# A shifted long convolution beside linear attention: four tap sums by adding DMA instead of two, and a new written-out order

## The chip, the core and the metric

The kernel runs on one core of a Trainium2 chip, and the metric is the device time of one execution in microseconds (us). A core has five engines that each work through a queue of their own in order: TensorE (PE, matrix products and transposes), VectorE (DVE), ScalarE (ACT), GpSimd (POOL) and SyncE (SP, which here only issues DMAs). They share an on-chip memory of 128 partitions (SBUF) and eight banks of accumulators (PSUM, here `ps_all`). Transfers between the chip's memory (HBM) and SBUF, or within SBUF, run on 16 DMA engines. They are issued on SP's queue or, where the transfer adds to its destination, on POOL's.

## The reference

Two independent functions of separate inputs, all in bf16, put side by side: the output is 2048 rows of 576 + 576 columns.

```python
# part A: inputs q, k, v (2048 x 576), shift_k (576 x 4), ssm_k (576 x 2048), ssm_D (576)
for t in range(4):
    k_shift = k_shift + k_pad[:, t:t+S, :] * shift_k[:, 3 - t]
kv = k_shift * v
y = irfft(rfft(kv, 2S) * rfft(ssm_k, 2S))[:S]        # causal convolution with a filter of 2048
y = y + kv * ssm_D
a = q * y
# part B: inputs x (2048 x 576), wqkv (576 x 1728), wo (576 x 576); 32 heads of 18
q, k, v = split(x @ wqkv)
phi = lambda t: where(t > 0, t + 1, exp(t)) + 1e-6
pq, pk = phi(q), phi(k)
kv = einsum("bhsd,bhse->bhde", pk, v);  z = sum of pk over s
num = pq @ kv;  den = pq . z + 1e-6
b = (num / den) @ wo
```

## The kernel before, in words

**Part A.** The 576 channels are worked on in three chunks of 192 (0, 1, 2), and the 2048 positions as 128 partitions of 16 neighbours, in two halves of 8. The shifted k of one chunk and one half is a *conv piece* (`conv_piece`, stages cv00 to cv21: the first digit is the chunk, the second the half). A piece is two tap products on DVE (L402, 3072 elements a partition each: a tap makes two of the four shifted products at once), a first sum that adds one tap's 3072 elements to the other's ("tap+"), a second sum of 1536, and the product with v ("tapv", 1536). The three after the taps are recorded as an operation of either VectorE or GpSimd (L236). For the pieces that the list `ACC` names, the first sum is instead a DMA inside SBUF that adds to its destination, issued by GpSimd (L408). All conv pieces of half 0 read k from the buffer kh0, those of half 1 from kh1, and multiply into v0 and v1.

The long convolution is a Fourier transform done in two matmul stages each way. First the filter: its rows hs0 to hs4 are loaded, transposed by PE ("htr") and evicted ("hev") into hT, with ssm_D added to the first sample ("hD"). For each chunk, "s1" multiplies by the table G (8 groups of 4 matmuls, L468), DVE or ACT evicts it, DVE transposes blocks of 32 ("tr"), "s2" is 4 groups of small matmuls (L516), evicted again. The chunk's three thirds are numbered 3*chunk + 0, 1, 2. kv goes the same way (s1u, s2u); then the two spectra are multiplied (p1, p2, on DVE or POOL, with X, a copy of the filter's spectrum with neighbouring partitions exchanged, made by two DMAs), "i1" (L552) and "i2" (L577) transform back with the table E, the result is evicted to yb, multiplied with q ("yq") and stored.

**Part B.** x is loaded in four groups, as rows (x_sb) and transposed (xT; group 0 by PE, groups 1 to 3 by transposing DMAs). "k r" (16 of them, L624) projects keys of 128 positions, ACT takes an exponential ("kexp", L629), and DVE joins it with the linear branch into pk ("kphi", L632). "q" (20 of them, L645) does the same for queries into pqT. G (10 groups, L674) is x transposed times pk; from it and the value weights follow per head kv (L709, masked by DVE at L712, "kvev") and the sums z, "den" and their reciprocals, which are stored to HBM ("rw") and loaded back spread over partitions (rb), and multiplied into pqT ("pqn", L236). M is kv times wo ("M", evicted at L231; a correction for the 1e-6 in "msf" and "msev"); "out" (32 groups, L814) multiplies pqT by M, is evicted and stored.

**The order.** Nothing is scheduled at build time. Every operation is recorded with a running number (838 in all), and two long strings fix the rest: `PLAN` gives the order of all of them with a letter for the engine, and `PLACES` the SBUF offset or PSUM bank of each of 473 buffers, so that buffers whose times don't overlap share a place, and the later one's first write waits for the earlier one's last reader.

```python
def _issue(P):
    names = dict(P="PE", A="ACT", D="DVE", G="POOL", S="SP")
    for w in PLAN.split():
        o = P.ops[int(w[1:])]
        o.eng = names[w[0]]
```

So D84 is operation 84 on DVE, and G84 would be the same on POOL. Each engine takes its own operations in this order, and an instruction that waits holds up all behind it on its engine. SP keeps some eight of its DMAs under way. One rule is added at the end: a two-input operation (`two=1`: sums and products) on POOL waits for the last such operation that stands before it in `PLAN` on DVE, so that these don't run at once.

Numbers that are spoken of later: loads 54 and 53 (the tail of the key weights wk, 72 KB, and their main part), 56 and 55 (of the query weights wq), 18 (srow, the tap weights), 26 and 28 (x group 0), 41, 46, 51 (transposed x), 58 to 60 (kh0), 62 (kh1), 61 and 63 (v0, v1), 365, 371, 423, 472, 478 (hs0 to hs4); 27, 29, 39, 44, 49 (the copies "x4c" of x columns); the conv pieces

| piece | taps | first sum | second sum | tapv |
|---|---|---|---|---|
| cv00 | 64, 65 | 66 | 67 | 68 |
| cv01 | 69, 70 | 71 | 72 | 73 |
| cv10 | 74, 75 | 76 | 77 | 78 |
| cv11 | 79, 80 | 81 | 82 | 83 |
| cv20 | 84, 85 | 86 | 87 | 88 |
| cv21 | 89, 90 | 91 | 92 | 93 |

95 + 3r, 96 + 3r, 97 + 3r (projection, exponential and kphi of key block r: P110, P116, P134 and D121, D130, D136, D139 are such), 143 to 202 the same for queries (D163, P182), 203 to 227 G, 228 to 245 kv, z, den, 246 to 271 the reciprocals' way, 272 to 284 M, msf and msev, 285 to 364 out, 365 to 526 the filter's transform (P507 is an s2 of chunk 2), 527 to 763 kv's transform and the products (P697 is an s1 of chunk 2), 764 to 835 i2 and the end.

Of the kernel before, what the change touches and what calls it, by code (L numbers as in the profile page):

```python
# [22 lines left out]
YA = [0, 1]  # L23
XD = [1, 2, 3]
HDT = []
ACC = [(0, 1), (2, 1)]
HP = [0, 128, 256, 384, 480, 576]


# [154 lines left out]
def kernel(  # L184
# [39 lines left out]
    def load(name, b, fn, nb, row, wr=None, rd=(), after=(), engs="S"):  # L224
        return P.op(engs, fn, rd=rd, wr=[b] if wr is None else wr, name=name, after=after, nb=nb, row=row)
# [165 lines left out]
    def conv_piece(cc, bh):  # L391
# [12 lines left out]
        for i in (0, 2):  # L404
            P.op("D", lambda e, i=i: tap(e, i), rd=[kh, (Wj, 0)] + ([(Wj, 1)] if cc else []), wr=[(m, i)], name="tap",
                 n=3072, x2=1, two=1, st=st)
        if (cc, bh) in ACC:
            load("acc", m, lambda e: nc.gpsimd.dma_start(  # L408
# [459 lines left out]


PLAN = """  # L870
G8 D836 P837 G5 G57 S26 G13 S28 G6 D27 S16 S54 S53 G3 P30 D29 D31 G11 G7 P36 P32 S21 S365 G1 G9 A33 S371 S20 G2 P34
P98 S423 D35 S19 P95 P368 G0 D37 A15 A99 A369 S18 S41 P366 D100 G228 D367 P101 P375 A96 S472 D97 P372 A102 A377
A374 D376 P394 G4 D373 S59 D370 A395 P386 P392 D103 G10 G14 P384 P426 D387 A393 P424 G12 S56 G378 D385 A23 D427
P388 A425 P433 D379 G42 A434 P435 P382 S55 G428 D389 D436 P390 P380 P437 D391 A383 P443 D438 A381 P429 D405 P475
P441 A444 P431 D414 S24 S40 S58 P473 A430 A442 D396 P439 A432 A440 S60 P146 P417 A147 P415 S25 A474 G477 D476 D445
A418 P104 D148 A105 P143 S46 P401 P397 A416 P446 P448 S51 D106 P452 A144 P155 A449 A453 A398 D454 A402 P149 P152
A156 A150 D145 A447 S478 P408 D463 G47 D157 A153 P403 P399 P457 D151 A409 D400 S50 S45 P468 P170 A458 A404 P406
D469 P410 P461 D154 A462 D65 P459 P421 P161 A171 A411 P158 S48 A460 P412 S43 P466 P455 G52 D172 P419 D64 A407 A422
P164 D75 A456 P481 D74 D66 P470 A413 A467 P464 S230 P450 A420 P167 A165 G67 A451 A471 A162 D163 P479 A465 A480 A168
P197 D166 P200 A482 P191 A159 A192 D169 A201 D160 A198 D202 D193 P110 P185 D76 A111 G44 G483 D112 D199 P173 S594  # L880
A186 P134 P176 A174 G49 S61 D175 D187 A135 P122 A177 P179 G77 D178 D136 P107 S652 P119 A123 D124 A180 A108 P137 D78
D85 S229 A120 P188 D109 D181 A138 S595 D121 G68 S232 A189 P140 P128 S38 A141 D139 D190 P125 D84 A129 D142 P131 D130
P486 D86 P116 A126 A487 A132 A117 D127 P113 G87 S231 A114 S62 A39 S653 D133 D118 P194 P494 P182 D115 A183 P223 D88
A224 P484 A485 A195 D70 D79 A495 P226 A225 S17 P208 D69 D80 A227 S63 P236 D237 D238 P203 G71 D184 P239 D196 P243
P488 G81 D204 A209 A205 A210 P492 D240 D241 S552 D244 P498 A489 P206 D242 D245 A493 P490 A499 D72 D73 A491 P496
S553 S246 P218 A497 S247 A207 D219 P537 D220 A538 P531 S259 P529 A530 P221 P533 D82 S260 S258 P527 A532 A222 S254
D83 A534 P535 D89 A536 S261 P213 A528 P618 S265 P620 P608 P211 D90 A621 P610 A609 P606 D255 A212 D619 D266 A611
P614 D214 S269 G91 G270 P216 A607 D500 S252 P503 A215 P507 G262 A615 D518 P519 D509 P612 D217 A504 D508 P616 A520
D92 S263 S674 P541 P233 A613 P539 A617 A542 S271 A540 D93 P699 D235 P281 G272 D234 S267 P693 D700 P275 D694 A282
P273 P279 A276 A274 P277 D280 S248 A278 P691 A692 P685 P695 P283 D622 A696 S256 D686 P687 D284 S673 P629 P516 G253  # L890
A688 P627 P514 D517 P697 G264 D564 A630 P689 G268 A698 P332 A333 P347 A628 P355 A690 D664 G249 P357 P350 A356 A515
A351 P667 P669 D348 P671 A358 D585 S250 D701 A672 S631 P521 P512 G251 P505 P330 P352 A670 P327 P325 A513 A331 A668
D522 D353 A328 P665 D506 S573 P510 S574 D743 S22 P706 A326 P625 S329 P525 A666 P501 A511 P623 D643 A624 G257 P300
P345 S359 A707 P340 A626 P342 A341 A526 P302 P750 P704 P748 D502 P648 S354 G675 S632 A346 D301 P590 A343 D722 P650
G676 D705 D591 P362 S711 A649 D363 P360 P312 P567 A303 D651 A749 P565 A751 S731 P644 A361 S732 P523 D313 P646 A568
P744 S349 P708 A524 P315 D543 S753 D316 P310 P337 P317 D647 P569 A745 D311 S334 P586 D634 P725 A566 A645 S304 D655
P571 P723 A709 A338 P727 S364 A318 A728 P290 A726 S344 A587 P320 P683 A321 P307 A570 S319 A572 S314 D724 P729 P746
D291 A684 P702 P550 P548 D654 A703 P677 A747 P305 P660 P681 A306 A308 A661 D633 P641 S752 A682 P292 A551 P658 A293
A549 A659 P335 A642 D576 P679 A680 P297 A678 P635 D730 P546 P592 P544 D754 D755 D733 A336 S710 P588 D734 D713 A636
A593 A589 P756 P637 D712 A545 P295 A638 P639 A640 D298 P656 P737 A657 P739 A740 P662 A547 A738 A663 P741 P718 P720  # L900
P758 A721 P760 A759 P762 D757 P800 A801 A761 P735 D575 D555 S294 S94 P794 D296 A795 P796 D597 P802 D763 S339 A742
P577 D719 A803 A797 A736 D596 P806 S309 P716 P788 P714 A717 D554 P579 D804 A807 D798 P322 P808 A715 P824 P826 P790
S299 A323 D825 P832 A789 A791 P600 S324 P560 A809 A601 S799 A827 P581 A833 P812 P562 D792 P598 A599 D578 P814 D582
A561 D815 P830 A580 G810 G828 A563 S793 D813 P583 A584 D831 D816 S805 P558 P820 D821 G834 D559 P602 P556 S811 P818
P604 P285 D819 D603 A557 S829 S835 A605 D822 S817 D286 S823 P287 A288 S289 P784 P782 D785 A783 D786 P776 S787 A777
P778 A779 P772 D773 D780 S781 P764 P770 P766 D767 A771 D774 S775 A765 D768 S769
"""
PLACES = """
# [16 lines left out]
"""  # L925


# [28 lines left out]
```

## Time and profile before

| | |
|---|---|
| median of 3 runs | 160.50 us (160.44, 160.50, 160.75) |
| profiled execution | 161.04 us, of which the span of engine work is 159.2 us |
| mean granted TensorE clock | 0.994 |
| HBM read, written | 20.86 MB, 4.99 MB: 162 GB/s over the span |
| adding DMAs (GpSimd's queue) | 1.57 MB, 5.6% of the 16 DMA engines' span |

The profile is of one execution. Its first part gives each engine's busy time, its share of the span and its instructions; a stage is a stretch of the span that I chose by its bounds, written start:end and followed by its length and the busy time in it. The groups of instructions are listed by code line, engine, operation, output and inputs, with count, total busy time and the mean of one in ns. In the chain, each entry is a start, a time and the instruction. The busy time of PE is no proof that it is the limit at each place, because an engine that is nearly always busy can still start its work late; that is why stages and chain are read beside it. SPq and POOLq are the queues' issuing of a DMA.

### The profile page before, as it was taken

To read this page: it belongs to the slowest core of one execution; us is meant where nothing else is said; L and a number is where in the kernel's file an instruction comes from. 1 tells how busy PE (TensorE), PEld (TensorE's weight loads), DVE (VectorE), ACT (ScalarE), POOL (GpSimd) and SP (SyncE) were. 2 spreads that over 40 slices of the span, in tenths; PEclk is the share of its full clock that TensorE was granted. 3 is DMA by queue.
4 is the path that set the end of the run, shared out by engine and by line. 5 is a ranking of instruction groups with operands and counts; after the bars stand their busy time and mean duration, and the time that the engine had idled before them with its cause. 6 is when DMAs were issued, how large, how long until landed. Compare 5 with 4: busy or idle time off the path is not lost.

```text
span 159.2 us, 4176 instructions
## 1 busy us (share of the span) xinstructions
PE 150.4 (94%) x1663; PEld 119.5 (75%) x1663; DVE 143.3 (90%) x183; ACT 122.7 (77%) x224; POOL 63.2 (40%) x51
## 2 busy tenths in 40 slices
PE   6897899999999999999999999999999999999970
PEld 2686785545677889787888878787777889999960
DVE  1537999999999999899899999999999999998981
ACT  3148799999996566561869599899989999896860
POOL 8901100110199170606920594996891000004400
PEclk9999999999999999999999999999999999999997
DMA  5999699999999128496925597891647449415575
GB/s 164 301 401 291 155 218 377 214 200 277 397 371 302 31 36 296 197 252 213 164 81 183 155 161 234 268 368 67 245 171 252 174 120 408 178 43 161 151 211 148
DMA packets 26317, 34.37 MB, mean 216 GB/s; under 512 B 15802, under 2 KB 20923, under 8 KB 25530
## 3 DMA queue, kind: packets, MB, share of 16 engines
q1 hardware_dynamic: 25754, 32.54, 65.8%
q0 software_dynamic: 544, 1.57, 5.6%
q8 instruction: 13, 0.21, 0.5%
q14 instruction: 6, 0.05, 0.1%
HBM read 20.86 MB, written 4.99 MB: 162 GB/s over the span
## 4 chain that ended last, share of the span: by engine, by line
PE 82%; DVE 5%; DMA 3%; ACT 3%; issue 2%; SPq 1%; DVEq 1%; ACTq 0%
PE ps_all L645 13%; PE ps_all L814 13%; PE ps_all L624 12%; PE ps_all L674 12%; PE ps_all L552 10%; PE ps_all L468 9%; PE ps_all L516 5%; PE ps_all L577 4%; DMA wk<-in_B_wqkv_dram 3%; DVE Cu L231 2%; PE ps_all L437 2%; SPq L222 1%; ACT sph L229 1%; PE ps_all L709 1%; DVE q L236 1%
## 5 line engine op out<-in xcount | busy, mean ns | idle before, releaser
L645 PE MATMUL ps_all<-xT,wq 128*126 128x512 bf16 (+1 forms) x100 | 24.0, 381 | 0.1
L814 PE MATMUL ps_all<-M,pqT 126*128 126x288 bf16 (+1 forms) x160 | 22.1, 287 | 0.0
L236 POOL TENSOR_TENSOR m<-m 128x1536 bf16<-128x1536 bf16 (+1 forms) x4 | 15.5, 3885 | 15.4 <-DVE m L236 15.4
L624 PE MATMUL ps_all<-wk,xT 128*128 128x288 bf16 x160 | 21.1, 286 | 0.5 <-DMA wk<-in_B_wqkv_dram 0.5
L402 DVE TENSOR_TENSOR m<-kh,Wj 128x3072 bf16<-128x3072 bf16 x12 | 20.5, 1752 | 0.1
L624 PEld LDWEIGHTS <-xT 128*128 128x128 bf16 x160 | 17.4, 109 | 3.6 <-issue 0.8
L814 PEld LDWEIGHTS <-pqT 126*128 126x128 bf16 (+1 forms) x160 | 16.8, 110 | 3.8 <-issue 2.0
L468 PEld LDWEIGHTS <-Gsb 128*128 128x128 bf16 x192 | 16.1, 98 | 4.2 <-issue 2.2
L645 PEld LDWEIGHTS <-wq 128*126 128x126 bf16 (+1 forms) x100 | 12.6, 131 | 7.9 <-issue 1.7
L552 PE MATMUL ps_all<-Esb,sph 128*128 128x128 bf16 x144 | 18.0, 219 | 0.0
L552 PE MATMUL ps_all<-Esb,X 128*128 128x128 bf16 x144 | 17.9, 219 | 0.0
L236 POOL TENSOR_TENSOR pqT<-pqT,rb 126x1024 bf16<-126x1024 bf16 (+1 forms) x8 | 16.8, 2138 | 2.5 <-DMA rb<-r_scr 2.1
L229 ACT ACTIVATE spu<-ps_all 128x512 bf16<-128x512 f32 x30 | 17.0, 636 | 0.6 <-PE ps_all L516 0.6
L229 ACT ACTIVATE Cu<-ps_all 128x768 bf16<-128x768 f32 x20 | 15.7, 853 | 2.0 <-PE ps_all L468 2.0
L229 ACT ACTIVATE V<-ps_all 128x512 bf16<-128x512 f32 x29 | 16.4, 661 | 1.2 <-PE ps_all L552 1.2
L674 PE MATMUL ps_all<-pk,x_sb 128*128 128x289 bf16 (+1 forms) x128 | 17.1, 287 | 0.0
L629 ACT ACTIVATE ek<-ps_all,neg 128x576 bf16<-128x576 f32 x16 | 11.7, 740 | 6.5 <-PE ps_all L624 6.4
L229 ACT ACTIVATE Ch<-ps_all 128x768 bf16<-128x768 f32 x18 | 14.2, 855 | 3.1 <-PE ps_all L468 3.1
L229 ACT ACTIVATE sph<-ps_all 128x512 bf16<-128x512 f32 x29 | 16.1, 625 | 0.3 <-PE ps_all L516 0.3
L648 ACT ACTIVATE eq<-ps_all,neg 126x512 bf16<-126x512 f32 (+1 forms) x20 | 13.7, 708 | 2.9 <-PE ps_all L645 2.6
L552 PEld LDWEIGHTS <-sph 128*128 128x128 bf16 x144 | 14.1, 98 | 0.7 <-issue 0.5
L674 PEld LDWEIGHTS <-x_sb 128*128 128x128 bf16 x128 | 12.3, 98 | 2.9
(97 smaller groups left out, 299.8 us busy)
## 6 DMA issues: line engine op xcount, KB each, us to landing
X<-sph SPq DMA_DIRECT2D x18, 256.0 KB, 4.7
v<-in_A_v_dram SPq DMA_DIRECT2D x2, 1152.0 KB
out_dram<-ob SPq DMA_DIRECT2D x16, 144.0 KB, 2.1
q<-in_A_q_dram SPq DMA_DIRECT2D x1, 2304.0 KB
out_dram<-q SPq DMA_DIRECT2D x12, 192.0 KB, 2.5
rb<-r_scr SPq DMA_DIRECT2D x8, 252.0 KB
x_sb<-in_B_x_dram SPq DMA_DIRECT2D x3, 576.0 KB
kh<-in_A_k_dram SPq DMA_DIRECT2D x1, 1584.0 KB
```

The source lines that it names most:

```text
L229: nc.scalar.activation(out=o, in_=i, func=ACTF.Copy)
L236: return (nc.vector if e == "DVE" else nc.gpsimd).tensor_tensor(out=o, in0=a, in1=b, op=op)
L402: return nc.vector.tensor_tensor(out=m.t[:, i:i + 2], in0=i0, in1=i1, op=ALU.mult)
L468: nc.tensor.matmul(ps.t[:, bank, lo - 384 * bank:hi - 384 * bank], lhsT=Gsb.t[:, b, ri, :], rhs=src[:, lo - CC * j:hi - CC * j], start=Tru ...
L516: nc.tensor.matmul(ps.t[32 * j:32 * j + 32, 0, :], lhsT=W2()[32 * kh:32 * kh + 32, :], rhs=ct.t[32 * kh:32 * kh + 32, 8 * j:8 * j + 8], st ...
L552: nc.tensor.matmul(ps.t[:, 0, 128 * c:128 * c + 128], lhsT=src.t[:, 4 * hh + c, :], rhs=Esb.t[:, 32 + wi, :], start=(wi == 0), stop=(wi == 1))
L624: nc.tensor.matmul(ps.t[:, hh, 0:HALF], lhsT=cols(xT.t[0:KT[t], t, :], r), rhs=wk.t[0:KT[t], t, HALF * hh:HALF * hh + HALF], start=(t == 0 ...
L629: P.op("A", lambda e: nc.scalar.activation(out=eb.t[:], in_=ps.t[:, :, 0:HALF], func=ACTF.Exp, bias=neg1.t[:]), rd=[ps, neg1], wr=[eb], na ...
L645: nc.tensor.matmul(ps.t[0:hn, 0, :], lhsT=wq.t[0:KT[t], t, h0:h0 + hn], rhs=xT.t[0:KT[t], t, :], start=(t == 0), stop=(t == 4))
L648: P.op("A", lambda e: nc.scalar.activation(out=eb.t[0:hn], in_=ps.t[0:hn, 0, :], func=ACTF.Exp, bias=neg1.t[0:hn, :]), rd=[ps, neg1], wr=[eb],
L674: nc.tensor.matmul(ps.t[0:m, 0, 0:n], lhsT=x4[r // 4].t[:, r % 4, :] if t == 4 else x_sb[r // 4].t[:, r % 4, 128 * t:128 * t + 128], rhs=p ...
L814: nc.tensor.matmul(ps.t[:, 0, 0:HALF], lhsT=cols(pqT[r // 8].t[0:kn, c, 512 * (r // 4 % 2):512 * (r // 4 % 2) + 512], r), rhs=M.t[0:kn, c, ...
```

## The change

`ACC` grows from two pieces to four: the first sums of cv20 and cv11 are now made by adding DMAs too, so operations 81 and 86 move from VectorE or GpSimd to a transfer. Operation 86 was a sum of 3072 on VectorE, 81 one on GpSimd. Both strings are replaced: the order of all operations, the engine of those that may run on more than one, and all places.

```diff
-ACC = [(0, 1), (2, 1)]
+ACC = [(2, 0), (0, 1), (1, 1), (2, 1)]
...
 PLAN = """
-G8 D836 P837 G5 G57 S26 G13 S28 G6 D27 S16 S54 S53 G3 P30 D29 D31 G11 G7 P36 P32 S21 S365 G1 G9 A33 S371 S20 G2 P34
-P98 S423 D35 S19 P95 P368 G0 D37 A15 A99 A369 S18 S41 P366 D100 G228 D367 P101 P375 A96 S472 D97 P372 A102 A377
...
+D836 P837 G13 G0 S28 G10 S26 S18 S16 G7 G1 S53 A15 G2 G3 S54 A23 S21 S371 G5 G29 A27 P30 P36 D31 S365 P32 A33 D37
+P34 D35 S20 P98 A99 G6 P95 P375 D100 D376 P101 G228 S423 S19 A96 A102 P372 D377 P368 S56 P366 A374 D97 G9 S24 A367
...
```

What changes by engine, worked out from the two strings:

- SP, the first loads, before: 26 28 16 54 53 21 365 371 20 423 19 18 41 472 59 56 55 24 40 58 60 25 46 51 478. After: 28 26 18 16 53 54 21 371 365 20 423 19 56 24 472 41 55 59 40 25 58 60 46 45 51 50 43 478. So srow (18) goes ahead of idw (16), wk's tail (54) behind its main part (53), and wq's two loads and the tap weights' way over HBM (24, 25) move forward. After the G stage the order is 63 246 247 230 260 259 254 265 261 269 271 267 263 ...: the reciprocals' stores and loads first, and most X loads behind them.
- POOL, its larger work, before: 67 44 483 49 77 68 87 71 81 91 270 262 272 253 264 268 249 251 257 675 676 810 828 834, where 81 is a sum of 3072 and 71 and 91 are adding transfers. After: 77 78 49 39 86 483 67 68 88 81 71 82 91 270 262 92 257 249 253 251 675 676 828 816, where 86, 81, 71 and 91 are adding transfers 39 a copy that ACT had before; 44, its like, goes to ACT in return, and 27 and 29, those of x group 0, leave DVE for ACT and POOL.
- DVE no longer has the sum 86, two of its tapv and some evictions; it gains two pqn products. ACT takes two of the last yb copies from DVE.
- Places: kh0 goes to 95616 and kh1 to the same 95616, where before they had 17536 and 117184. So kh1's load 62 waits for the last tap that reads kh0, which in the new order is D84 (DVE's new order there is D85 D84 D127 D139 D142 D133 D115 D118 D136 D87 D130 D121). Of POOL, G86 (the transfer of cv20) waits for D84 and D85, and D87 for G86.

More of the change, by code (lines that the diff above doesn't have):

```diff
@@ L876 @@
[L876 to L895, printed above, removed]
@@ new lines @@
+A432 D405 P439 P443 A444 G4 A440 D414 P104 P473 A105 P437 P441 S58 S60 S46 D474 S45 P143 D106 G477 P419 P410 D396
+P415 A438 A442 P417 P408 A144 P406 A407 A416 A409 G47 D445 P149 A411 D145 A420 P152 P146 P421 G14 A153 P452 D454
+A418 S51 P450 P161 D463 S50 P155 A147 A150 A422 D453 A162 D148 P446 P461 P397 A451 D154 P412 A156 P448 D151 D163
+D157 P158 P466 A398 A447 S43 A449 P401 D75 A413 A467 P164 G52 P399 A462 A165 P403 P455 A404 A456 P470 A471 P167 D74
+D166 P173 A159 A402 P185 P468 A400 A168 P459 P464 D64 A465 D65 A469 D76 P176 P191 A186 A177 A460 D178 D160 A44 P197
@@ new lines @@
+A174 P170 D169 D175 A192 G77 P194 P107 D193 S478 P481 A198 S61 P479 S48 A171 D172 P179 A195 D66 A108 S38 D109 P122
+D187 S229 S231 G78 D199 A480 A180 A123 P125 D196 A482 D181 D124 A126 D85 D84 P137 A138 G49 D139 D127 P188 P140 P200
+G39 G86 A201 A141 P116 A189 P131 A132 A117 D142 D190 D202 G483 D133 P113 P110 S62 P134 A114 D115 A111 D112 A135
+P128 P490 D118 P119 G67 G68 D136 D87 G88 P496 A129 D130 A491 P486 A120 P182 D121 A497 D487 P488 P484 A485 A183 P226
+D80 P498 A489 A499 P223 P213 S232 A224 P492 D79 A225 D70 D227 A493 S17 A214 S63 P236 P494 D184 D69 G81 D238 G71
@@ new lines @@
+D237 P221 P239 P457 A495 D518 P243 A215 P523 P519 A524 P525 A526 D240 D241 D242 P218 A219 S246 A220 A458 S247 P203
+A204 D244 G82 D245 S230 P606 D520 A222 D83 D72 D73 P616 S260 A617 P216 A217 P612 P206 A613 P620 A607 D509 A205 P610
+A611 D89 A621 P208 D90 P693 A207 P685 A686 A694 S259 S254 P529 D255 S265 P211 S261 D500 S269 A530 G91 D266 D209
+P505 P503 P501 A212 G270 G262 D210 A504 P507 D508 G92 A506 D502 P521 D522 P233 D234 P531 P618 S271 S267 S263 P614
+A532 D235 P535 P279 D619 P539 A615 P273 D536 S653 S248 S256 A280 S252 P527 S710 D540 P537 D538 A274 P533 S250 P277
@@ new lines @@
+A528 S752 A534 P275 P281 D278 P687 P608 A276 A688 P541 D282 D93 P283 D268 P699 S258 S673 S674 S711 A609 P514 D284
+A542 S574 A700 P689 A690 P697 P691 S553 D264 S753 D643 S652 P350 A515 P352 A698 G257 D664 A692 P357 S594 P695 A358
+S573 P347 P340 S552 A696 D622 A353 S631 S22 P355 D351 A348 P644 A341 A356 S359 P648 D543 A649 A645 P512 D743 A513
+P665 D666 P671 P667 P669 P330 A670 P342 P335 A343 A336 D331 P332 P744 P650 P748 A672 P550 P625 D668 A333 G249 A749
+S354 D564 D722 D651 A626 P646 P337 A338 A745 P362 A363 A551 G253 G251 P345 D701 P325 P327 A346 P725 P727 P723 D585
@@ L907 @@
+P598 D813 G816 P305 A599 A306 D603 P824 S823 D825 S817 S309 P784 S829 D785 P782 P764 A783 D786 S787 A765 P766 A767
+D768 S769 P770 P772 A771 A773 D774 S775 P778 P776 A777 A779 D780 S781
 """
 PLACES = """
[16 rows of a table removed]
[16 rows of a table added]
 """
```

26 lines of the change are left out of this document (12 added, 14 removed), and 32 rows, old and new, of the table PLACES.

## The prediction, before the changed kernel was run

> **What bounds the kernel now.** I read the page's part 1, then the busy time by stage, then the chain that ended last.
>
> ```profile
> PE 150.4 (94%) x1663; PEld 119.5 (75%) x1663; DVE 143.3 (90%) x183; ACT 122.7 (77%) x224; POOL 63.2 (40%) x51
> ...
> 7.89:39.00 31.11, 29.52 (x317) 20.53 (x317) 27.53 (x36) 27.03 (x46) 3.02 (x8) 1.00 1.03 264
> 39.00:97.28 58.28, 58.28 (x539) 47.28 (x539) 56.64 (x66) 41.25 (x66) 28.81 (x13) 1.00 0.68 207
> 97.28:104.30 7.02, 6.84 (x73) 5.27 (x72) 6.95 (x11) 6.56 (x11) 6.71 (x4) 1.00 0.85 250
> 104.30:152.17 47.87, 47.86 (x688) 41.34 (x687) 46.15 (x63) 44.00 (x96) 17.44 (x8) 1.00 0.55 192
> ...
> 2.76 5.09 DMA wk<-in_B_wqkv_dram
> 10.51 0.99 PE ps_all L437 x16
> 11.50 1.24 PE ps_all L624 x10
> 50.89 1.08 PE ps_all L645 x5
> 61.62 0.33 PE ps_all L468 x4
> 77.79 1.97 PE ps_all L674 x16
> 95.83 1.45 PE ps_all L709 x25
> 98.20 1.63 DVE Cu L231 x2
> 102.67 0.77 DVE M L802
> 107.46 0.76 PE ps_all L516 x24
> 122.99 0.45 PE ps_all L552 x8
> 123.44 0.62 PE ps_all L814 x5
> 139.88 0.33 PE ps_all L577 x4
> ```
>
> Columns of the stages after their length: PE, PEld, DVE, ACT, POOL busy. TensorE sets the end; it starts real work when wk lands (2.76+5.09). The chain gives its pace: a key projection 1.24, a query projection 1.08, G 1.97, out 0.62, i1 0.45, s1 and i2 0.33, an h transpose 0.50, s2 0.127. Times their counts (16, 20, 10, 32, 36, 48+24, 10, 72) that is 135; with kv 1.45 and about 4 of small ones 140.3. From 7.89 it would end at 148.2; it ends at 154.1 (a row below). So PE runs 6 us late. Counted likewise, the work before 39.00 (4 k, 9 q, 16 s1, 24 s2, 9 transposes) is 27.4 of 31.1: 3.7 late there. From 39 to 97.28 nothing is added (the second stage is all PE), about 1.1 comes at 97 to 104, where the chain goes over VectorE, and 1.2 in hair gaps behind. VectorE works 56.64 of 58.28 in stage two. The order is written out, so DVE's queue decides how late PE is: whatever DVE needs longer than PE for its work up to a given matmul, plus DVE's own idle time.
>
> ```profile
> 10.18 0.76 DVE L632 SCALAR_TENSOR_TENSOR pk<-ek,ps_all 128x576 bf16<-128x576 bf16 x1 [1.83 <-ACT ek L629]
> 60.07 1.42 DVE L632 SCALAR_TENSOR_TENSOR pk<-ek,ps_all 128x576 bf16<-128x576 bf16 x2
> 85.04 3.43 DVE L402 TENSOR_TENSOR m<-kh,Wj 128x3072 bf16<-128x3072 bf16 x2
> L236 DVE TENSOR_TENSOR m<-m 128x3072 bf16<-128x3072 bf16 x3 | 5.2, 1748 | 0.0
> L236 DVE TENSOR_TENSOR m<-m 128x1536 bf16<-128x1536 bf16 x3 | 2.8, 934 | 0.1
> L236 DVE TENSOR_TENSOR v<-m,v 128x1536 bf16<-128x1536 bf16 x5 | 4.8, 956 | 0.6 <-POOL m L236 0.5
> L236 DVE TENSOR_TENSOR pqT<-pqT,rb 126x1024 bf16<-126x1024 bf16 x2 | 1.4, 682 | 0.0
> L231 DVE CAST Cu<-ps_all 128x768 bf16<-128x768 f32 x4 | 3.7, 940 | 0.0
> L231 DVE CAST sph<-ps_all 128x512 bf16<-128x512 f32 x7 | 4.7, 676 | 0.1
> L231 DVE CAST M<-ps_all 126x576 bf16<-126x576 f32 x1 | 0.8, 758 | 0.0
> L712 DVE TENSOR_TENSOR kvb<-ps_all,cst 126x504 bf16<-126x504 f32 x1 | 0.7, 668 | 0.0
> L236 POOL TENSOR_TENSOR m<-m 128x1536 bf16<-128x1536 bf16 x3 | 9.3, 3095 | 15.4 <-DVE m L236 15.4
> ```
>
> Two kphi in a row take 1.42 where one takes 0.76: back to back, an instruction costs some 0.08 less than its mean.
>
> **The start (+0.1).** srow goes ahead, wk's tail behind wk. wk's own issue starts about 0.1 earlier, but the 72 KB tail now lands last: 72/576 of the some 3.4 us that wk's bytes take is 0.4, formerly in a stretch with room. Between -0.1 and +0.3; I take +0.1. The weights of the taps come sooner and SP no longer waits for the ACT copy of srow, so wq and xT1 are issued up to 5 us earlier. Nothing waits for them now (PE's early rows wait for wk and hT), so 0; the moved x, v and hs4 loads keep several us before their users. X loads go behind the reciprocal's stores, for products that start after 115: 0, but see the second rival.
>
> **DVE's load (early part -0.9).** DVE loses a 3072 sum (1.67), one 1536 sum on balance (0.9), two tapv (1.9), two x4c copies in its idle time, three out and some other evictions; it gains two pqn (1.2). Net some -5.8, POOL gains 11. Off the path where PE is the later one, so what counts is the latest pair. Old: PE reaches P110 after 32.2 (4 k, 13 q, 16 s1, 24 s2, 10 transposes) from 7.89, DVE the qphi D163 that frees its bank after 31.3 from 10.18: 1.4 behind, and DVE idles about 2.1 in between (31.11 less 27.53, less the 1.83 before 10.18, and handovers): 3.5, the trace 3.7. New: the worst pair is P116 (44.7 of PE work) and D139 (43.3 of DVE's): 0.9. Idle time I put at 1.9, since hT's evictions come first and s1 can start some 0.5 earlier. So PE is 2.8 late instead of 3.7. Bounds: 0 and -1.9 (all but wk's wait gone).
>
> **The first new transfer (+2.2).** This decides. kh1 now has kh0's place in SBUF, so its load waits for the last tap on kh0, D84; before, it waited for POOL's tapv. The adding transfer G86 waits for the same D84. And D87, on DVE, waits for G86.
>
> ```profile
> 58.56 0.33 SPq L222 DMA_DIRECT2D kh<-in_A_k_dram  x1
> 61.00:62.00 1.00, 1.00 (x12) 0.94 (x10) 1.00 (x2) 0.24 (x2) 0.00 (x0) 1.00 1.06 406
> 63.00:64.00 1.00, 1.00 (x11) 0.92 (x10) 1.00 (x3) 1.00 (x2) 0.70 (x1) 1.00 0.90 342
> 74.00:75.00 1.00, 1.00 (x10) 0.79 (x9) 1.00 (x5) 0.00 (x0) 1.00 (x2) 1.00 0.08 19
> 75.00:76.00 1.00, 1.00 (x47) 0.74 (x49) 0.78 (x3) 0.34 (x1) 1.00 (x1) 1.00 1.10 194
> 78.00:79.00 1.00, 1.00 (x11) 0.80 (x9) 1.00 (x2) 1.00 (x3) 1.00 (x1) 1.00 1.00 181
> m<-m POOLq DMA_DIRECT2D x2, 768.0 KB, 6.5
> 89.05 1.21 POOL L408 DMA_DIRECT2D m<-m  x1 [8.58 <-DVE m L402]
> ```
>
> The last two columns of the stages are DMA share and GB/s. kh1 alone keeps the 16 engines full from some 0.5 after its issue for 5.2. An adding transfer lands 6.5 after its issue, and in 75 to 79 it fills all engines too (share 1.00 to 1.10), 4.2 of those 6.5; POOL issues it 0.6 after the tap ends (89.05 against 85.04+3.43). New D84 ends at 10.18 + 42.6 + 1.9 = 54.7. Alone, G86 would land at 55.3+6.5 = 61.8, before DVE gets to D87: the kphi D136 ahead of it needs P134, which PE ends at 61.5, then an exponential, so about 63.0. Beside kh1 the work adds: from 55.2, 5.2 for kh1, 4.2, and up to 0.8 for the constants and wo's tail issued behind kh1, then 0.4 to land: 65.0 to 66. No row shows two queues at once, so the bounds are 61.8 (nothing shared: cost 0) and 66. I take 65.6, since each of the two fills the engines alone and kh1 is ahead by 1.5. Behind D87 stand kphi D130 and D121; P182 needs the bank that D130 frees: 65.6+0.95+0.67+0.1 = 67.3. PE has 54.4 of work up to P182, place 62.3: 5.0 late instead of 2.8.
>
> The Trainium skill (DMA: Bandwidth & Descriptors, Queues, rings and completion order) says each DMA engine takes turns between its queues, a packet at a time. By that rule both slow each other and the shorter packets end last, about 65.5 here; no run so far shows it.
>
> **The other three transfers (0).** cv11, cv01 and cv21 are shifted alike. D69 to D72 leaves 7.3 for 6.5; G82 (3.1) ends about when D83 comes; from D90, 0.6+6.5+3.1 = 10.2 for G92, against 10.4 of DVE work to D93. DVE also waits for den's matmul in between, which absorbs hundreds of ns. No cost taken; up to +1.0 from cv21.
>
> **The kv stage (-0.4).** New DVE order behind P507: three s2 evictions (1.83), kvev (0.74), four s1 evictions (3.5), two M evictions (1.36), tapv (0.95), pqn (0.6), msev (0.76): 9.8, and 0.3 of handovers. PE has up to P697, whose bank msev frees, 3 s2, kv, 13 s1, 5 M and msf: 8.2. So 1.9 more, and 0.1 for cv21: 2.0. Then DVE is ahead: each later pair I compared leaves PE at least 0.3 of room. Before, 1.1+1.2 arose here: -0.3 to -0.4. Bounds -1.5 (stall hidden) and +0.6.
>
> **The tail (-0.4).**
>
> ```profile
> 151.34 2.80 PE L577 MATMUL ps_all<-V,Esb 128*128 128x192 bf16 x32
> 154.65 1.02 DVE L236 TENSOR_TENSOR q<-yb,q 128x768 bf16<-128x768 bf16 x2
> ```
>
> Two yb copies move from DVE to ACT; the last product then follows PE's last matmul (154.14) by an ACT copy 0.5 and 0.56, some 1.15, and not 1.53. Bounds 0 and -0.6.
>
> **Sum.** Lateness 5.0+2.0 = 7.0 instead of 6.1: +0.9; start +0.1; tail -0.4: +0.6. The profiled run took 161.04 (span 159.2, the rest lies around it), 0.54 above the median 160.5; so 159.8 and 161.6, and for the median 161.1.
>
> **Rivals.** *The transfer is hidden* (faster): if G86 lands by 63.0, PE stays 2.8+2.0 = 4.8 late, -1.3+0.1-0.4 = -1.6: 158.9. For: DVE waits for PE there anyway. Against: both fill the engines. The point from which the sign turns is a landing at about 65.0. *Balance*: it lands at 64.8 to 65.2: 160.2 to 160.8. *The last chunk's transfer too* (slower still): rb loads and X loads, now issued beside G91, delay it by 1 to 1.7; G92 and D93 then hold msev up: 161.1+1.0 = 162.1; POOL's 3.1 adds leave it no room. *The change does not do what it says*: the evictions on DVE are off the path and nothing moves; then 160.5, within the balance.
>
> **Chances.** Forecast 0.45, last chunk too 0.12, balance 0.10, hidden 0.33. Range 158.4 to 162.4: the hidden case less 0.5 (the early part's bound of -1.9 instead of -0.9, and half of it spent again later) at one end, the second transfer's with 0.3 of measurement at the other; cases of both signs are in it, the forecast's own range is 160.8 to 161.7. A measurement of this kernel tells about 0.2% (0.3 us) from no change. Faster 0.33, same 0.10, slower 0.57.
>
> **What would show it.** Right: kh1's issue and the POOL transfer within 1 us of each other near 55; the first transfer over 9 us to landing where the others take 6.5; a DVE wait of 2 to 3 us on it before a 1536 sum; a PE pause of about 2 us near 65 and one of 1.9 near 100; DVE busy about 137. Wrong: a landing in 6.5 to 8 us, then the second case; PE pauses before 40 as long as now; wk's landing moved by more than 0.3; or POOL waits holding up tapv products near 80.

## The result and the profile after

The changed kernel takes 168.07 us (median of six, 167.38 to 169.49) against 160.91 us of the kernel before, measured again (median of six): a ratio of 1.045, 95% interval 1.042 to 1.048. It is slower, as forecast, but by 7.2 us and not by 0.6, and the time lies far outside the range of 158.4 to 162.4. Medians here and below are of all executions of a run, ratios leave out those that took over 1.5% longer than the fastest of their kernel, and the profile of the first order under "The waiter moved back on VectorE" is of such a longer one.

The profiled execution is the slowest of the six (169.49 us, span 167.7). From its page: the engines' busy time, the granted clock in 40 slices, and the adding transfers' median time to landing.

```profile
PE 152.4 (91%) x1663; PEld 119.2 (71%) x1663; DVE 138.0 (82%) x174; ACT 123.6 (74%) x230; POOL 61.4 (37%) x54
...
PEclk9999999999999999957999999999999999999998
...
m<-m POOLq DMA_DIRECT2D x4, 768.0 KB, 7.6
```

VectorE works 5.3 us less than before, as the count of operations said, and the kernel is slower: its share of the span falls from 90% to 82%. The stages of the changed kernel (columns as in the prediction) say where:

```profile
8.07:39.00 30.93, 29.55 (x300) 20.55 (x300) 26.85 (x35) 26.63 (x44) 6.89 (x14) 1.00 1.08 273
39.00:66.00 27.00, 27.00 (x205) 21.29 (x204) 23.28 (x28) 19.91 (x32) 14.53 (x8) 1.00 0.73 226
66.00:72.00 6.00, 0.15 (x2) 0.13 (x1) 1.81 (x3) 0.84 (x2) 0.78 (x1) 0.90 0.64 234
72.00:80.00 8.00, 8.00 (x44) 5.58 (x44) 6.44 (x5) 2.99 (x4) 3.54 (x2) 0.65 0.00 0
103.00:113.00 10.00, 9.57 (x103) 7.87 (x104) 9.82 (x15) 8.73 (x14) 5.40 (x3) 1.00 1.01 278
```

PE does next to nothing from 66 to 72, where it was busy without a gap before, and from 72 to 80 it is busy without a gap at a mean granted clock of 0.65. By the clock's own record it was 0.50 from 70.8 to 77.6, and 1.00 before and behind that up to the last matmul, so that PE's work from 71.9 to 77.6 took 5.7 us where 2.9 would have done. The chain of work shows what stands there:

```profile
52.19 3.35 DVE m L402 x2
...
56.14 13.96 DMA m<-m
...
70.19 0.13 DVE m L236
...
71.06 0.76 DVE pk L632
...
71.87 2.29 PE ps_all L645 x5
74.16 1.28 PE ps_all L468 x8
75.44 3.09 PE ps_all L674 x16
```

This is the place that the prediction named: tap D84, transfer G86, sum D87, kphi D130, query projection P182. The transfer takes 14 us from its issue, where those of the kernel before took 6.5. Behind it a query projection takes 2.29 us and not 1.08, a group of G 3.09 and not 1.97. From the timeline, the issues of kh1, of the transfer and of v1, and D87:

```profile
55.59 0.33 SPq L222 DMA_DIRECT2D kh<-in_A_k_dram  x1
...
56.14 1.35 POOL L408 DMA_DIRECT2D m<-m  x1 [3.89 <-DVE m L402]
...
62.65 0.33 SPq L222 DMA_DIRECT2D v<-in_A_v_dram  x1
...
70.19 0.96 DVE L236 TENSOR_TENSOR m<-m 128x1536 bf16<-128x1536 bf16 x1 [5.93 <-DMA m<-m]
```

And what each DMA queue moved in three stretches of it (packets, MB, share of the 16 engines; q0 is the adding transfer's queue, q1 that of SP's loads). From 57.5 to 61:

```profile
q1 hardware_dynamic: 86, 1.09, 97.5%
```

From 62.5 to 66, and from 66 to 70.1, when v1's packets are there:

```profile
q0 software_dynamic: 186, 0.57, 83.8%
q1 hardware_dynamic: 171, 0.22, 21.3%
...
q1 hardware_dynamic: 189, 1.24, 73.0%
q0 software_dynamic: 71, 0.17, 21.4%
```

POOL had issued the transfer by 57.5, but not one packet of it ran before 61: the engines were full with kh1. Its first packet ran at 61.1, when 25 of kh1's 128 packets had not started yet. Then it had most of the engines until v1 came.

Counted as in the prediction (work since the first key projection at the chain's prices, with 0.7 us more for the small ones), PE is late by 3.7 us before and 3.6 after at 45; by 3.3 before and 12.2 after at 92; by 5.2 before and 13.7 after at its last matmul. So 8.8 us arise between 66 and 80 (5.8 of standing still, 3.0 of slow clock), and nothing else of size.

### The profile page after: what moved, and what is told of

Read it like the earlier page. It is cut to its first block, busy times and chain, and to the rows that moved or that the text cites. A ratio compares the mean times of both kernels' runs of the same rounds, so it can differ in the third digit from the quotient of the medians.

```text
span 167.7 us, 4157 instructions
## 1 busy us (share of the span) xinstructions
PE 152.4 (91%) x1663; PEld 119.2 (71%) x1663; DVE 138.0 (82%) x174; ACT 123.6 (74%) x230; POOL 61.4 (37%) x54
## 4 chain that ended last, share of the span: by engine, by line
PE 76%; DMA 11%; DVE 6%; ACT 2%; issue 1%; SPq 1%; ACTq 0%; DVEq 0%; POOLq 0%
PE ps_all L645 13%; PE ps_all L674 12%; PE ps_all L814 12%; PE ps_all L552 10%; DMA m<-m 8%; PE ps_all L468 8%; PE ps_all L516 5%; PE ps_all L577 5%; PE ps_all L624 4%; DMA wk<-in_B_wqkv_dram 3%; PE ps_all L437 3%; DVE m L402 2%; SPq L222 1%; DVE pk L632 1%; PE ps_all L709 1%
## 5 line engine op out<-in xcount | busy, mean ns | idle before, releaser
L645 PE MATMUL ps_all<-xT,wq 128*126 128x512 bf16 (+1 forms) x100 | 24.7, 394 | 5.8 <-DVE pk L632 5.8
L229 ACT ACTIVATE Ch<-ps_all 128x768 bf16<-128x768 f32 x19 | 15.2, 845 | 12.6 <-PE ps_all L468 11.9
L468 PEld LDWEIGHTS <-Gsb 128*128 128x128 bf16 x192 | 16.6, 100 | 4.3 <-issue 2.9
L229 ACT ACTIVATE sph<-ps_all 128x512 bf16<-128x512 f32 x30 | 16.6, 622 | 2.9 <-PE ps_all L516 2.9
L229 ACT ACTIVATE V<-ps_all 128x512 bf16<-128x512 f32 x31 | 18.2, 667 | 0.3 <-PE ps_all L552 0.2
L629 ACT ACTIVATE ek<-ps_all,neg 128x576 bf16<-128x576 f32 x16 | 11.7, 742 | 7.1 <-PE ps_all L624 7.0
L236 POOL TENSOR_TENSOR m<-m 128x1536 bf16<-128x1536 bf16 x4 | 12.8, 3196 | 10.1 <-DVE m L236 8.1
L229 ACT ACTIVATE spu<-ps_all 128x512 bf16<-128x512 f32 x28 | 15.8, 630 | 0.0
L632 DVE SCALAR_TENSOR_TENSOR pk<-ek,ps_all 128x576 bf16<-128x576 bf16 x16 | 11.7, 750 | 4.1 <-ACT ek L629 4.0
```

Source lines behind the costliest of these rows:

```text
L229: nc.scalar.activation(out=o, in_=i, func=ACTF.Copy)
L236: return (nc.vector if e == "DVE" else nc.gpsimd).tensor_tensor(out=o, in0=a, in1=b, op=op)
L468: nc.tensor.matmul(ps.t[:, bank, lo - 384 * bank:hi - 384 * bank], lhsT=Gsb.t[:, b, ri, :], rhs=src[:, lo - CC * j:hi - CC * j], start=Tru ...
L629: P.op("A", lambda e: nc.scalar.activation(out=eb.t[:], in_=ps.t[:, :, 0:HALF], func=ACTF.Exp, bias=neg1.t[:]), rd=[ps, neg1], wr=[eb], na ...
L632: P.op("D", lambda e: nc.vector.scalar_tensor_tensor(out=pk[r // 4].t[:, r % 4, 0:D].rearrange("p (h c) -> p h c", h=2), in0=eb.t[:], scal ...
L645: nc.tensor.matmul(ps.t[0:hn, 0, :], lhsT=wq.t[0:KT[t], t, h0:h0 + hn], rhs=xT.t[0:KT[t], t, :], start=(t == 0), stop=(t == 4))
```

## Experiments

The theory: G86, issued behind kh1's load and beside it, lands late, VectorE waits for it with kphi behind it, and PE stands still. The rivals: that the new order costs it as a whole; that the transfer is slow by itself; that the slow clock is the larger part.

### The sum back on VectorE

```diff
-ACC = [(2, 0), (0, 1), (1, 1), (2, 1)]
+ACC = [(0, 1), (1, 1), (2, 1)]
-G86 ... D87
+D86 D87
```

> The changed kernel with the sum 86 back on VectorE, just ahead of D87; the other three transfers and everything else stay. Theory (the one new transfer beside kh1's load causes the loss: 5.8 us of idle PE and some 3 us of slow clock behind it): VectorE pays 1.75 us for the sum, PE stays at full clock, 160 to 162 us. Rival (the new order as a whole costs it, the transfer only shows where): at least 165 us.

Measured: 162.68 us, ratio 1.013 (1.007 to 1.019), just above the expected 160 to 162 and far from the rival's 165. PE's longest waits in the stretch become this one:

```profile
PE ps_all L645 <- DVE pk L632: 1.6, 1, 1.6
```

The clock is 1.00 from 64 to the last matmul. So 5.4 of the 7.2 us belong to this one transfer. What is left is 1.3%: PE loses 1.8 us at P182, where VectorE now has the 1.75 of the sum in front of D87.

### kh1's load after the transfer

```diff
+# in the loop that issues: operation 62 waits for the landing of 86
```

> The changed kernel with one wait more: kh1's load is issued when the transfer 86 has landed. Theory: the transfer lands 6.5 us after its issue (at about 62.6), VectorE doesn't wait at D87, kh1 lands near 69 and its first tap waits about 1 us; 159 to 161.5 us. Rival (the transfer is slow by itself here, for instance because POOL works meanwhile): it still lands 10 us or more after its issue and the time stays at 165 or more.

Measured: 163.09 us, ratio 1.011 (1.006 to 1.016).

```profile
63.53 0.33 SPq L222 DMA_DIRECT2D kh<-in_A_k_dram  x1
...
64.03 0.95 DVE L236 TENSOR_TENSOR m<-m 128x1536 bf16<-128x1536 bf16 x1
...
69.97 1.76 DVE L402 TENSOR_TENSOR m<-kh,Wj 128x3072 bf16<-128x3072 bf16 x1 [2.31 <-DMA kh<-in_A_k_dram]
```

The transfer, issued at 56.02, landed at 63.4, 7.4 after its issue, and D87 waits no more. POOL works meanwhile as it did, so its work isn't what slows the transfer. The price is kh1's own lateness: its first tap waits 2.3 us, more than the 1 us expected, and the time is 1.6 us above the upper end of the expected range. The two small loads behind kh1 on SP's queue (wo's tail and the constants) are issued later with it, here and in every run that delays kh1.

### kh1's load just behind the transfer's issue

```diff
+# operation 62 waits for POOL's instruction 483, which stands behind G86
```

> The changed kernel with kh1's load issued only behind POOL's small instruction 483 that follows the transfer's issue, so about 2 us later than in the changed kernel and just behind the transfer in time. If what is issued first is served first: the transfer lands in 6.5 to 7.5 us and the time is near that of the run in which kh1 waits for the landing. If the two queues take turns packet by packet: each of kh1's rows of 12672 bytes goes between two of 3072, the transfer lands 10 to 11 us after its issue, near 67, and the time is 163 to 166.

Measured: 166.62 us, ratio 1.032 (1.024 to 1.041). The transfer landed 11.7 us after its issue, at 67.7, and PE stood 3.6 us: a little later than the second case of the expectation has it, and far from the first. By queue, from 57.9 to 61 and from 61 to 66.5:

```profile
q0 software_dynamic: 161, 0.49, 103.9%
...
q1 hardware_dynamic: 127, 1.61, 69.7%
q0 software_dynamic: 109, 0.29, 33.5%
```

Now it is kh1 that has no packet until 61.6, 4.0 us after its issue (before, where nothing was in its way, its first packet came 0.95 us after its issue). Once both are under way they move as many packets each, 44 and 44 from 62 to 64, and a packet of kh1 is four times as large (rows of 12672 bytes against 3072). The Trainium skill (DMA: Bandwidth & Descriptors, Queues, rings and completion order) has engines take turns between queues, a packet at a time, and says that a packet is typically 9 to 17 descriptors. The equal counts from 62 to 64 agree with that. The 3 to 4 us ahead of them would agree only if what the profile counts as a packet is one descriptor: the 161 packets here and the 86 in the changed kernel are some 10 and 5 for each of the 16 engines. No run tells whether it is so.

### v1's load held back

```diff
+# operation 63 waits for the landing of 86
```

> The changed kernel with v1's load, which was issued at 62.65, held until the transfer 86 has landed; kh1 stays as it is. Theory (kh1 holds the transfer until 62, v1 its last packets from 66 on): lands near 67 instead of 70.1, 2.5 to 3 us less idle, 164 to 166 us. Rival (kh1 alone does it): lands at 69.5 to 70 as before, no change from 168.

Measured: 167.3 us, ratio 1.039 (1.033 to 1.046). The landing moved from 70.1 to 68.9:

```profile
68.95 0.96 DVE L236 TENSOR_TENSOR m<-m 128x1536 bf16<-128x1536 bf16 x1 [4.69 <-DMA m<-m]
```

So v1 costs 1.2 us of the landing and kh1 with the small loads behind it the rest. The landing was expected near 67 and the time at 164 to 166; the gain, some 0.8 us, lies within the two intervals.

### PE kept busy while it waits

```diff
+    for j in range(23):   # ahead of P182, into a free bank, read by nothing
+        nc.tensor.matmul(fp2.t[:, 0, :], lhsT=Gsb.t[:, 0, 0, :], rhs=..., start=True, stop=True)
```

> The changed kernel with 23 products of 128x512 that nothing uses (some 5 us, into a free accumulator bank) put ahead of P182, where PE otherwise stands still from 66.8 to 71.8. The wait on the transfer is as long as in the changed kernel. Theory (the idle time is also what takes the clock away): the granted clock stays at 1.00 from 70 to 80, q there takes 1.1 and not 2.3, G 1.97 and not 3.09, some 2.9 us are gained: 165 to 165.5 us. Rival (the clock falls for another reason, or the slow products are another wait): the rows stay slow and the time stays near 168.

Measured: 169.83 us, ratio 1.051 (1.043 to 1.059), and not 165. Two of its stages:

```profile
75.00:80.00 5.00, 5.00 (x45) 4.06 (x43) 5.00 (x5) 2.41 (x5) 1.22 (x1) 1.00 0.02 3
...
100.00:116.00 16.00, 13.97 (x126) 10.78 (x126) 14.07 (x19) 12.06 (x19) 10.31 (x5) 0.89 1.01 284
```

The first half of the expectation holds: the clock stays at 1.00 from 70 to 80, and at 92 PE is 9.4 late and not 12.2. The second half falls: nothing is gained in the end. The chain from 95 on shows why:

```profile
97.91 8.58 DMA m<-m
...
106.55 3.11 POOL m L236
...
109.68 0.96 DVE v L236
```

This is the last chunk's transfer (G91, G92, D93), and P699 waits for it; in the changed kernel it ran at nearly the same time, hidden behind a PE that was still later. VectorE's 5.9 us of waiting have probably gone into this chain too, through its taps. P699 waits 1.4 us for it, and behind that pause the clock is 0.50 from 112.2 to 115.6, which costs another 1.7. So the 3 us that the clock no longer took were lost again at the next wait.

### The kernel before with this transfer alone

```diff
-ACC = [(0, 1), (2, 1)]
+ACC = [(2, 0), (0, 1), (2, 1)]
```

> The kernel before with one edit: its sum 86 becomes an adding transfer at the same place in the order; order, places and all else as before. kh1's load is issued at 58.56 there too, the transfer near 60.2, and G87 on POOL waits for it, then D88. Theory (it is the meeting of the two transfers, not the new order): the transfer needs 10 us or more, D88 waits for G87 until about 73 instead of 66.4, VectorE and then PE stand 4 us: 163 to 166 us. Rival (a transfer for the sum is good by itself, VectorE saves 1.75 us): 159 to 160.5 us.

Measured: 169.82 us, ratio 1.055 (1.049 to 1.062). From its waits:

```profile
POOL m L236 <- DMA m<-m: 10.4, 1, 10.4
...
DVE v L236 <- POOL m L236: 9.7, 1, 9.7
```

In the old order, where kh1 is issued 2.2 us ahead of the transfer, that one edit costs more than the whole change, and more than I expected. The transfer's first packet comes 4.1 us after the end of its issue, when kh1's last has started, and it lands 11.7 us after its issue, 5.2 later than alone. So the loss doesn't need the new order. But not all of it is the meeting: D88 waits for the transfer and for GpSimd's sum of 3.1 us behind it, and with a landing after 6.5 us it would still have waited some 4.4 of its 9.7 us (an estimate from these rows).

### kh1's load in four pieces

```diff
-load("kh1", ... [[16 * D, 128], [1, 11 * D]])
+for a in (0, 3, 6, 9): ... [[16 * D, 128], [1, (min(a + 3, 11) - a) * D]]
```

> The changed kernel with kh1's load cut into four DMAs of 3, 3, 3 and 2 rows, so that its packets are 3456 or 2304 bytes instead of 12672; the same bytes at the same place in the order. If a queue that comes second waits for a number of packets that the other has already brought forward, and takes turns from then on: the transfer's first packets come near 59 instead of 61, it lands near 66, 163 to 165.5 us. Rival (it waits for kh1's bytes whatever their packets): lands at 69 to 70, 167 to 168.5 us.

Measured: 167.42 us, ratio 1.039 (1.034 to 1.044); the transfer lands at 69.0. From 57.5 to 61 only kh1's queue moves, with 356 packets where it was 86:

```profile
q1 hardware_dynamic: 356, 1.12, 101.7%
```

So what the second queue waits for isn't a number of packets; the bytes are the same, 1.1 MB in 3.5 us. Three of the four pieces were issued ahead of the transfer's descriptors, and when its first packet ran, at 61.4, all but 13 of their 384 packets had started; the fourth piece then shared with it. The rival was right.

### The waiter moved back on VectorE

```diff
-D136 D87 G88 ... D130 ... D121 ... D487 ... D80 ... D79 ... G81
+D136 ... D130 ... D121 ... D487 D80 D79 G81 D87 G88
```

The places of the shifted products of cv01 and cv11 are exchanged too.

> The changed kernel with the waiting sum D87 (and G88 behind it) moved behind D130, D121, D487 and the two taps of cv11 (80, 79) on VectorE, with the places of the two shifted products of cv01 and cv11 exchanged so that these taps don't wait for G88. The transfer is as late as ever (69 to 70). Theory (what costs is not the late transfer but what stands behind its waiter, kphi that free PE's banks): PE doesn't stop near 66, it is 3.5 late there and 5.4 at the end: 160 to 162 us. Rival (the sums behind cv20 and cv11 are needed so soon that the wait only moves on): a wait of several us before a tapv or s1 of the second chunk, 164 us or more.

Measured: 167.75 us, ratio 1.041 (1.035 to 1.046), by its time the rival's case. Nothing that PE needs at once stands behind D87 now, and PE passes 66 to 72 without a gap; it then stops at z:

```profile
PE ps_all L723 <- DVE GT L687: 4.0, 1, 4.0
...
DVE m L402 <- POOL v L236: 3.5, 1, 3.5
```

D70 now waits for G88, which waits for D87, and D227 behind it is what z needs. A second run put D70 behind what PE needs:

```diff
-D70 D227 ... D184 D69 D238 G71 D237
+D227 ... D184 D238 D237 D70 D69 G71
```

> The run with the waiting sum moved behind the taps of cv11, where D70 then waited 3.5 us for G88 with D227 and the evictions of z (237, 238) behind it; here D70, D69 and the transfer 71 stand behind these three. If the stop at z (4.4 us of PE) came from that order alone: PE reaches 85 some 4 us less late, 163 to 165 us. If VectorE's lost time as such sets the end (it stands idle for the late transfer, wherever the wait is put): 166.5 or more, the loss comes back later, at a tapv or at an s1 of chunk 1 or 2.

Measured: 165.55 us, ratio 1.028 (1.025 to 1.031), above the expected range of the first case, below that of the second. PE stops 2.1 us later on and then runs slowly, 32 matmuls of G in 6.8 us:

```profile
80.73 0.64 PE L516 MATMUL ps_all<-ct,idw 32*32 32x512 bf16 x12 [2.08 <-DVE dcol L754]
81.37 6.80 PE L674 MATMUL ps_all<-pk,x_sb 128*128 128x289 bf16 x32
```

A third order moved D69 and its transfer behind D518 and the steps of den too:

```diff
-D70 D69 G71 ... D518 ... D240 D241 D242
+D70 ... D518 ... D240 D241 D69 G71 D242
```

> The last order (the waiting sum behind the taps of cv11, D70 behind the evictions of z) with the second tap of cv01, D69, and its transfer 71 moved behind D518, D240 and D241. In the run before it PE stood 2.1 us at P523, which needs D518, and then ran 32 products of G in 6.8 us instead of 3.95. If these are the loss (the pause 2.1, the slow clock that came after it 2.9) and the late transfer itself costs nothing once nothing that PE needs stands behind its waiter: 160.5 to 162.5 us. If VectorE's lost time sets the end all the same: 164.5 or more, with waits at the tapv and s1 of chunks 0 and 2.

Measured: 168.88 us, ratio 1.053 (1.045 to 1.061), by its time the second case. The stop at 80.7 shrinks to 0.4 us, and the next ones are larger, 1.4 us at 83.8 and 4.1 us at 87.8: 71 lands at 88.8, D72 waits for it, and a group of G follows late and slow. That D72's wait is what holds the eviction (ACT Cu) that this group waits for is not shown; for ACT's wait of 7.1 us ahead of it the profile names no cause. VectorE's row and PE's:

```profile
88.85 0.96 DVE L236 TENSOR_TENSOR m<-m 128x1536 bf16<-128x1536 bf16 x1 [2.23 <-DMA m<-m]
```

```profile
91.86 3.61 PE L674 MATMUL ps_all<-pk,x_sb 128*128 128x288 bf16 x16 [4.11 <-ACT Cu L229]
```

Three orders, three places of the stop. Moving a waiter back doesn't make its transfer land sooner, and each stop is followed by slow matmuls. That a better order could hide it is not excluded by these three.

### The sum in a gap, and kh1 between the two extremes

On VectorE (with `ACC` as in the first experiment) the sum can stand ahead of D142, where VectorE was idle:

```diff
-G86 ... D142
+D86 D142
```

> The changed kernel with the sum 86 on VectorE, this time ahead of D142, where VectorE stood idle 0.97 us (and 0.5 and 0.4 us at the two kphi after it) in the run with the sum ahead of D87. If what that run still lost against the kernel before (1.9 us, of them 1.8 at P182) is the 1.75 us of the sum in a place where PE waits for VectorE: PE loses about 0.5 at P182, 161.2 to 162 us. If the loss belongs to the new order itself: 162.5 or more, as there.

Measured: 163.55 us, ratio 1.012 (1.006 to 1.017): no better than the sum ahead of D87. In the profile the stretch around P182 loses 0.9 us and not 1.8, but a load of a filter row came late at 11 us (an h transpose waits 0.5 for hs), and PE was 0.6 later at 45 already, so this pair is inconclusive. With the places of the two products exchanged as well:

> As the run with the sum in the gap, and the places of the shifted products of cv01 and cv11 exchanged, so that D80 doesn't wait for G88 (1.0 us in the changed kernel and in the runs made from it) but the taps of cv01 may. If that wait was on the path: 0.3 to 1.0 us faster than with the sum in the gap alone. If not: the same, or slower where D70 now waits in front of D227.

Measured: 162.51 us, ratio 1.008 (1.006 to 1.010). D80's wait is gone, PE is late by 6.5 us at the end and not by 7.5 (7.15 with the sum ahead of D87). The direction is that of the expectation; the times of the two runs overlap.

The best of all is the changed kernel with kh1's load issued at 60.6:

```diff
+# operation 62 waits for D133
```

> The changed kernel with kh1's load issued behind D133, near 60.4: 3 us later than in the run where it followed POOL's issue (57.5) and 3 us earlier than in the one where it waited for the landing (63.5). If the queue that comes second gets its first packet some 3.5 us after its issue and then takes turns: kh1's packets start near 63, when the transfer is all but done, which lands at 63.4 to 64.5; kh1 lands about 1 us earlier than when it waits for the landing, D80 waits 1 to 1.5 us and not 2.3; 161.5 to 163 us. If they take turns from the issue on: the transfer lands at 65 or later and D87 waits.

Measured: 161.73 us, ratio 1.0003 (0.9966 to 1.0039): no difference from the kernel before that can be told by the ratio. Its ten executions spread more, though: five took 160.7 to 161.2 us and five 162.3 to 164.2, where all 13 of the kernel before took 160.8 to 161.7. The profile is of one of 162.26.

```profile
56.19 1.35 POOL L408 DMA_DIRECT2D m<-m  x1 [3.88 <-DVE m L402]
60.57 0.33 SPq L222 DMA_DIRECT2D kh<-in_A_k_dram  x1
...
69.30 3.43 DVE L402 TENSOR_TENSOR m<-kh,Wj 128x3072 bf16<-128x3072 bf16 x2 [1.46 <-DMA kh<-in_A_k_dram]
```

The transfer lands at 63.3. kh1's packets start at 62.3, 1.7 us after its issue and not 3.5, when all but two of the transfer's 256 had started. Delaying one load by 5 us takes the whole loss of the change away in half of the executions and most of it in the others. It is not faster than before. What waits last in it is the last transfer's chain (D93 0.95, P699 0.5 us), so its sum 92 was moved from POOL to VectorE:

```diff
-G92
+D92
```

> The run with kh1's load issued behind D133, and the last 1536 sum of cv21 (92) on VectorE (0.95 us) instead of POOL (3.1 us). There the last transfer landed at 100.03, G92 took until 103.2, and D93 waited 0.95 and P699 0.5 us. If this chain is what is left on the path: 0.5 to 1 us faster than there, 160 to 161 us, at or just below the kernel before. If VectorE has no room at that place: the same or slower.

Measured: 168.94 us, ratio 1.047 (1.039 to 1.056), the opposite of the first case. VectorE and what PE then waits for:

```profile
101.61 0.96 DVE L236 TENSOR_TENSOR m<-m 128x1536 bf16<-128x1536 bf16 x1 [4.27 <-DMA m<-m]
```

```profile
PE ps_all L468 <- DVE sph L231: 4.8, 1, 4.8
```

The transfer landed at about the same interval after its issue (8.0 us). With POOL as the waiter, VectorE waited 0.95 us; with VectorE as the waiter at this place it stood 4.3 us with evictions behind it, and a change of one letter costs some 7 us by the medians. In the profile some 5 of these come from this stop on (4.8 of standing still and a clock of 0.50 from 100.7 to 107.5); that execution also started PE 1.0 us later and had an early stretch at half the clock (8.5 to 11.9), which the letter has no visible part in. A place for D92 further back, just ahead of D93, wasn't tried.

## Why the prediction was right or wrong

**The place and the sign: right.** The point at which the forecast's case decides was a landing at 65.0; it was 70.1. Undoing that transfer alone takes 5.4 of 7.2 us away, moving kh1's load to 60.6 takes all of it by the ratio. So the cause is shown: the meeting of this transfer with kh1's load. A place of its own for kh1 in SBUF, so that it could be loaded earlier, wasn't tried.

**The start (+0.1): not decided.** PE's first key projection began at 8.07 and not 7.89, but in the profiles of the runs made from the changed kernel, whose first loads are the same, it began anywhere from 7.3 (the sum on VectorE) to 9.1 (sum 92 on VectorE). That the 0.18 here looks like the forecast is luck.

**The early part (-0.9): wrong.** PE was as late at 45 as before (3.6 against 3.7). D84 ended at 55.5 and not 54.7: VectorE started 0.2 later, its work up to there was 0.5 more than I summed, and its idle time was 2.0 and not 1.9. A difference of 0.9 between two sums of 43 us each was less than the sums were good for.

**The first new transfer (+2.2): the term that failed.** It came to +8.8. The step "5.2 for kh1, 4.2, and up to 0.8 for the constants and wo's tail" put the transfer's first packet at 60.4 and its landing at 65.6. That the transfer comes behind kh1 was right: its first packet ran at 61.1. What failed is the 4.2 (with up to 0.8) for the transfer itself. From its first packet to the end of its last it took 8.3 us (61.1 to 69.4), though its own packets filled the engines for only 4.0 of these (the shares above). The rest of the engines' time went to the end of kh1, to the small loads, and from 66 on to v1, which the step left out although it stands on SP's queue right behind the constants, and which is worth 1.2 us of the landing. So of the 4.5 us to 70.1, 0.7 are the later first packet, 3.5 the sharing, and 0.3 the way from the last packet to the landing. kh1's row was misread too: before, its packets began 0.95 us after its issue (59.5) and not 0.5, and ended at 65.2, 5.7 us later and not 5.2; in the changed kernel they ran for 6.8 us (56.5 to 63.3). I named 66 as the upper bound, and that bound had no row of two queues at once behind it. Of the +8.8, 5.8 are the pause and 3.0 the slow clock behind it, of which the prediction said nothing: a PE that stands still was priced at the time it stands. In the filled run these 3.0 were lost again later, at the last chunk's chain.

**The other three transfers (0, up to +1.0 from cv21): right for the changed kernel.** G91 landed 8.1 us after its issue, beside the rb loads, and PE didn't wait for what follows from it. But the reason was wrong: it was hidden because PE was late already. In the filled run P699 waits 1.4 us for it, with kh1 at 60.6 it waits 0.5; with kh1 after the landing no such wait is seen.

**The kv stage (2.0): about right in size.** From 92 to the end PE lost 1.5 us in the changed kernel and 1.9 with the sum on VectorE or kh1 after the transfer. Before lost 1.9 there by the same count, and not 2.3. So the -0.4 came out only where PE was late already, and the single pause of 1.9 that the step names was not seen: the longest in that stage is 0.3 in these three runs.

**The tail (-0.4): wrong, 0.** The last product still ends 1.52 us after PE's last matmul (163.76 + 0.56 against 162.80), as before. ACT's last copies do follow PE at once, but the product then starts 0.4 us after its copy has ended.

**The rivals.** *Hidden* would not have given 158.9: with the transfer on time (the run with kh1 at 60.6) the kernel is as fast as before. The -0.9 and the -0.4 are not there. So of my two largest chances, one had the right mechanism with a quarter of its price, and the other a time that the kernel can't reach in this order.

**What would show it.** The issues within 1 us of each other near 55, over 9 us to landing, and VectorE busy about 137 (138.0): as said. VectorE's wait of 2 to 3 us was 5.9, PE's pause of 2 was 5.8, and from 103 to 113 (the place of the one near 100) PE stood still 0.4 us in all.

## What to carry to other kernels

A transfer that replaces work of an engine takes over that engine's place in the queue of whoever waits for it: look up which loads of other queues are issued in the two or three us around it, all of them, and price it as sharing the engines with each of them. Put such a waiter where least stands behind it, or delay the load that can wait; here 5 us of delay for one load were worth the 4.5% by the ratio. Price a stop of PE with the slow stretch that may follow it. Where a wait stops PE at several places in a row, taking away one of them gains nothing until the chain behind the next one is shorter too.

## What the runs showed of the hardware

**Two queues.** A transfer that came second had no packet for a while, in both directions. In the changed kernel q0's first packet came 3.6 us after the end of GpSimd's issue (0.6 in the kernel before, with nothing in the way); with v1 held back it was 4.3 us, in the old order 4.1. Where kh1 was issued 1.4 us behind the start of GpSimd's issue, its first packet came 4.0 us after its own issue (0.95 before). Cutting kh1's rows into packets of a quarter of the size changed nothing in that. Then they took turns (186 packets of q0 and 171 of q1 from 62.5 to 66 in the changed kernel). It is not a fixed time: with kh1 at 60.6 it was 1.7 us. In most runs the second came when the first was nearly through: 25 of kh1's 128 packets had not started in the changed kernel, 8 with v1 held back, none in the old order, 2 of the transfer's 256 with kh1 at 60.6. But where kh1 followed the issue it came with 75 of the 256 left. What holds the second one back isn't shown; the runs only exclude the packets' size.

**The clock after a pause.** In the changed kernel a pause of 5.8 us was followed by a clock of 0.50 that lasted 6.8 us (70.8 to 77.6). Pauses of 4.6 and 4.7 us (v1 held back, kh1 in four) were followed by slow stretches too, one of 3.6 us was not, but one of 1.7 us later in that same run was, and so was one of 1.4 us in the filled run; one of 1.6 us with the sum on VectorE was not. So the length of one pause doesn't tell it. In each of these runs the clock in the slow stretch was 0.50, and the stretch lasted 6.8 us (changed kernel, kh1 in four) or 3.4 us (the other three). The Trainium skill (TensorE: Matmul & The Clock Gate, Part 1: The HAM clock gate) says that the gate looks at how busy PE was in a window of some 3.4 us that runs freely, so that the same work may meet it differently: the lengths of 3.4 and 6.8 us agree with that, and so does a pause of 3.6 us that passes, while why single pauses as short as 1.4 or 1.7 us were enough no run here shows.
